# Weight decoding in a fused top-k attention and gated feed-forward kernel: shifts and adds at other places of a slot, the first P@V a slot later, other load counts

## The chip, the cores and the metric

The kernel runs on one core of one Trainium2 chip. The metric is the device time of one execution in microseconds (us); the time of a kernel is the median of its runs. Engines are named as in the profile: PE (TensorE), DVE (VectorE), ACT (ScalarE), POOL (GpSimd) and SP (SyncE). ACT and SP also issue the DMA transfers here.

## The reference

Attention in which every query keeps only its 32 largest scores, followed by a feed-forward layer with the activation h cos(h):

```python
B, H, S, D = 8, 8, 576, 64;  top_k = 32
scores = q @ k.T / sqrt(D)                       # per batch and head
kth    = np.partition(scores, -top_k)[..., -top_k]
scores = np.where(scores >= kth, scores, -1e9)
attn   = exp(scores - max);  attn /= attn.sum() + 1e-9
x = (attn @ v) with heads side by side           # 4608 tokens x 512
h = x @ w_in                                     # 512 -> 2048
out = (h * cos(h)) @ w_out                       # 2048 -> 512
```

q, k and v are float32. `w_in` and `w_out` come as 64-bit floats and are turned into 32-bit ones on the chip.

## The kernel before, in words

**Units and slots.** A unit is 128 tokens and one pair of heads. There are 36 token blocks of 128 and 4 head pairs, so 144 units. The order of all instructions is written out by hand: each engine executes its own in the order in which the code emits them. A loop goes through slots; slot `i` searches the largest scores of unit `u = i` on VectorE, makes mask and exponentials of `w`, the unit before, writes out the unit two before (`send`: split into 16-bit halves on GpSimd, a write of `rows` to memory and a transposing read into `pT`, both on SyncE's queue) and, in every even slot, takes two units `z` (3 and 4 before) through attention times values ("P@V": `values` on TensorE, then `take_values`, L486, on VectorE, which normalises into `xT`). `pT` has three buffers. `LAST` is 140; the last four units go through `last_slot`, and a loop after it finishes the feed-forward work.

**Top-k.** The 576 scores of a row are folded into the larger and the smaller of two halves: `rest` on VectorE (L247) and `low` on GpSimd as sum minus larger (`fold_sum` L265, `fold_low` L274). For units in `BUSY`, `low` is made on VectorE instead (`fold_now`, L255). MAX8 (L352) and MATCH_REPLACE8 (L357) then pull out eight values at a time; round 3 ends a slot on VectorE.

**Scores.** `scores` (L226) of two units are made in one even slot, of one unit where a block crosses a batch; `scored` holds which. ScalarE takes them out of PSUM (`take_scores`, L236 and L237). L237 and P@V use the same PSUM tile `rim`.

**Weights.** The 32 chunks of weights (16 of `w_in`, 16 of `w_out`, 512 KB each as 64-bit floats) are loaded by `load_weights(n, queue)` into staging tiles and decoded in three steps: `decode_first` on ScalarE (L133, L136) at the end of a slot, `decode_second` on VectorE (a shift, L144), `decode_third` on GpSimd (an add, L154). A staging tile is free once the add is done. The counter `wq["ready"]` is the number of chunks whose adds have been emitted before the slot begins. Staging tiles share their seven buffers (`CHUNKS`, tag `g`) with the feed-forward tiles `g`; a load is put off when staged chunks and live `g` tiles would be more than seven. A few early chunks use spare buffers of the tag `x`.

**Feed-forward items.** The work of a token block is cut into 8 first-layer items (`ff1`: 8 matmuls, 16 records of L537, 256 columns of one PSUM bank `mm`) and 8 second-layer items (`ff2`: 2 matmuls, 4 records of L612, all eight accumulated into one bank `o`), 576 items in all. `feed(n)` emits up to n items where the slot calls it, three times a slot, as far as `credit` allows (5 a slot less 0.9 for each unit scored, at most 5.3 kept). Kinds alternate, two first-layer and two second-layer items in turn; when the kind whose turn it is may not go, the other goes and the alternation starts anew from it:

```python
            for kind in (ff["kind"], 1 - ff["kind"]):
                if (can_first, can_second)[kind]():
                    break
            else:
                return
            ...
            if kind != ff["kind"] or ff["half"]:
                ff["kind"], ff["half"] = 1 - kind, 0
            else:
                ff["half"] = 1
```

`can_first` asks for the block's `xT` (two ticks old; a tick is one call of `feed`) and for `wq["ready"]` to cover the chunks of `w_in`; `can_second` asks for gated `g` tiles that are two or three ticks old and for

```python
wq["ready"] >= NC * NF // FC + f + 2     # 16 + f + 2, f = 0, 2, ... 14
```

Both kinds take their PSUM bank from the tag `mm`, which has two buffers. Two first-layer items in turn (even and odd) fill one bank; ScalarE then takes it out (`take_first`: L551, L553) where `take_banks` stands in the code. A bank `o` stays open over its eight second-layer items and is taken out by L622. From a finished `g` tile, GpSimd (L573, L582), ScalarE (a sine, L592) and GpSimd again (`gate`, L599) make h cos(h).

**ScalarE's order in a slot.** In an odd slot from slot 12 on: sine, mask (L381, L383), finished banks, `take_scores`, exponentials (L391), and at the end of the slot finished banks again. In an even slot the exponentials stand ahead of `take_scores`. A sine and an exponential need different activation tables, so an odd slot loads a table twice.

Of the kernel before, what the change touches and what calls it, by code (L numbers as in the profile page):

```python
# [30 lines left out]
def kernel(  # L31
# [16 lines left out]
    NP = H // 2  # L48
# [43 lines left out]
        w_out.append(w)  # L92
        chunks.append((moe_w_out[f * P : (f + 1) * P, :], w))
    CHUNKS, XB = 7, 4
    BUSY = range(7, 12)
    ff = {"live": 0, "tick": 0, "now": 0, "credit": 0.0, "end": False, "kind": 0, "half": 0, "open": 0, "late": False}

    wq = {"next": 0, "loaded": deque(), "second": deque(), "third": deque(), "done": 0, "ready": 0}
# [4 lines left out]
    def load_weights(n, queue):  # L103
        for _ in range(n):
            i = wq["next"]
            if i >= len(chunks):
                return
            src, dst = chunks[i]
            if not DECODE:
                queue.dma_start(out=dst, in_=src)  # L110
                wq["next"] = wq["done"] = i + 1
                continue
            spare = i < 3 * XB and i % 2 == 1 and staged(1) < XB
            if spare:
                st = ffw.tile([P, CW, 2], I32, tag="x", name="st", bufs=XB)
            elif staged() + ff["live"] >= CHUNKS:
                return
            else:
                st = ffw.tile([P, CW, 2], I32, tag="g", name="st", bufs=CHUNKS)
            queue.dma_start(out=st.rearrange("p w i -> p (w i)"), in_=src)  # L120
            wq["loaded"].append((st, dst, int(spare)))
            wq["next"] = i + 1
# [16 lines left out]
    def decode_second(n):  # L139

        for _ in range(min(n, len(wq["second"]))):
            st, w, spare = wq["second"].popleft()
            wi = w.bitcast(I32)
            nc.vector.tensor_scalar(  # L144
                out=wi, in0=wi, scalar1=3, scalar2=None, op0=ALU.logical_shift_left
            )
            wq["third"].append((st, w, spare))
# [13 lines left out]
    units = []  # L161
    for t0 in range(0, B * S, P):
        parts = []
        for i, a in enumerate((t0, t0 + TAIL)):
            b, q0 = a // S, a % S
# [75 lines left out]
    def fold_high(u):  # L241

        s, sc = u["s"], u["sc"]
        if u["n"] not in BUSY:
            del u["sc"]
# [5 lines left out]
    def fold_now(u):  # L251

        s, sc = u["s"], u.pop("sc")
        u["low"] = work.tile([P, 2, HS], F32, tag="low", name="low", bufs=1)
        nc.vector.tensor_tensor(  # L255
            out=u["low"], in0=sc[:, :, 0:HS], in1=s[:, :, HS:S], op=ALU.min
        )

    def fold_sum(u):

        if not u["folds"]:
            return
        s = u["s"].bitcast(I32)
        u["low"] = work.tile([P, 2, HS], F32, tag="low", name="low", bufs=1)
        nc.gpsimd.tensor_tensor(  # L265
            out=u["low"].bitcast(I32), in0=s[:, :, 0:HS], in1=s[:, :, HS:S], op=ALU.add
        )

    def fold_low(u):

        if not u["folds"] or u["n"] in BUSY:
            return
# [19 lines left out]
    def topk_first(u, w):  # L292
# [5 lines left out]
        if u["folds"]:  # L298
            if u["n"] not in BUSY:
                fold_sum(u)  # L300
# [3 lines left out]
        if merges:  # L304
            merge_second(w)
        if u["folds"] and u["n"] in BUSY:
            fold_now(u)
        topk_round(u, 0, [lambda: bounds(w), lambda: distances(w)] if w else ())

    def topk_round(u, rnd, between=(), ahead=None):  # L310
        top, rest, lasts = u["top"], u["rest"], TOPK // 8 - 1
        end = TOPK - 1 - 8 * rnd
        at = top[:, :, end : end - 8 if rnd < lasts else None : -1, 0]
        if u["folds"]:
            search(
                at, rest[:, :, HS:S] if rnd == 0 else rest[:, :, 0:HS], rest[:, :, 0:HS], rnd < lasts,
                between if rnd < lasts else (),
            )
        else:
            search(at, u["s"] if rnd == 0 else rest, rest, rnd < lasts, between)  # L320
        if rnd < lasts:
            return
        del u["rest"]
        if u["folds"]:
            low = u.pop("low")
            for k in range(TOPK // 16):
                more = k < TOPK // 16 - 1
                if ahead and not more:
                    take_values(ahead)
                search(  # L330
                    top[:, :, 1 + 8 * k : 9 + 8 * k, 1], low, low, more,
                    () if more or rnd < lasts else between,
                )
# [10 lines left out]
    def merge_second(u):  # L344
        nc.vector.tensor_reduce(
            out=u["top"][:, :, TOPK - 1, 1], in_=u.pop("lesser"), axis=mybir.AxisListType.X,
            op=ALU.max,
        )

    def search(to, src, rest, more, between=()):  # L350
        for j in range(2):
            nc.vector.max(to[:, j], src[:, j])  # L352
            if between:
                between[j]()
        if more:
            for j in range(2):
                nc.vector.match_replace(rest[:, j], to[:, j], src[:, j], NEG)  # L357
# [39 lines left out]
    def sums(u):  # L397
        den = small.tile([P, 2], F32, tag="den", name="den")
        nc.vector.tensor_reduce(out=den, in_=u["den"], axis=mybir.AxisListType.X, op=ALU.add)
        u["den"] = den  # L400

    def reciprocal(u):
        u["rden"] = small.tile([P, 2], F32, tag="rden", name="rden")
        nc.vector.reciprocal(u["rden"], u.pop("den"))

    def both(u):
        return [lambda: sums(u), lambda: reciprocal(u)] if u else ()
# [71 lines left out]
    def take_values(us):  # L479
        blk, hp, n = block_of[us[0]["tok"]], us[0]["hp"], len(us)  # L480
        if "xT" not in blk:
            blk["xT"] = work.tile([P, NP, P], F32, tag="xT", name="xT", bufs=5)
        for i, u in enumerate(us):
            to, o, pT = blk["xT"][:, hp + i], room[0][:, i * P : (i + 1) * P], u.pop("pT")
            if u["paired"]:
                nc.vector.tensor_tensor(out=to, in0=o, in1=pT[:, 2 * NT + 1], op=ALU.mult)  # L486
            else:
                nc.scalar.copy(out=to, in_=o)
        blk["left"] -= n
        blk["tick"] = ff["tick"]  # L490
# [181 lines left out]
    LAST = NU - NP  # L672
# [7 lines left out]
    at_slot, at_once = {}, {}  # L680
# [7 lines left out]
    for n in range(NP, len(order)):  # L688
        i = last[order[n - 5]] if n >= 5 else 0
        load_at(max(i, 2 * NP + 2), load_qk, *order[n])  # L690
        i = last_values[order[n - 6]] if n >= 6 else 0
        load_at(max(i + 4 - i % 2, 2 * NP + 2), load_v, *order[n])

    for hp in range(NP):
        at_once[hp] = [(load_v, 0, hp)]
    for hp in range(2, NP):
        at_once[hp - 2].append((load_qk, 0, hp))

# [10 lines left out]
        transposes(x)  # L709

    def slot(i, u, w, x, z):
        n = (3, 4, 3, 2)[i] if i < NP else 2 if i < 2 * NP else 3
        if i < NP:
            for load, b, hp in at_once[i]:
                load(b, hp)
        load_weights(n, nc.sync if i < 2 else nc.scalar)
        if x:
            send(x)
        decoding = i < 3 * NP
        ff["late"] = False  # L720
        topk_first(u, w)
        fold_low(u)
        topk_round(u, 1)
        topk_round(u, 2)
        if decoding:
            sines(1)
            gate(1)
        decode_second(NP)
        decode_third()
        reduce_first()  # L730
        reduce_second()
        made = scored.get(i, [])
        if z:
            take_banks()
        feed(1)

        for m in made:
            scores(m)
        if z:
            values(z)  # L740


        late = len(made) > 0

        if i % 2 and not decoding:
            sines(1)
        if w:
            mask(w)
        take_banks()
        if w and late:  # L750
            exponentials(w)
        take_scores(units[i + 1])
        if w and not late:
            exponentials(w)
        topk_round(u, 3, both(w), z)
        ff["late"] = not decoding
        if i in at_slot:
            load, b, hp = at_slot[i]
            load(b, hp)
        gate(1)  # L760
        feed(1 if len(made) == 2 else 2)
        take_banks()
        decode_first(NP)
        reduce_first()
        reduce_second()
        feed(1 if len(made) == 2 else 3)
        if i == LAST:
            sines(1)
# [51 lines left out]
    for i in range(NU + 1):  # L820
        ff["end"] = i >= NU
        ff["credit"] = min(ff["credit"] + 5.0 - 0.9 * len(scored.get(i, [])), 5.3)
        ff["now"] += 1
        wq["ready"] = wq["done"]
        u, w = (units[i - n] if 0 <= i - n < NU else None for n in range(2))
        x = units[i - 2] if 0 <= i - 2 < LAST else None
        z = units[i - 4 : i - 2] if i % 2 == 0 and 0 <= i - 4 < LAST else None
        if i <= LAST:
            slot(i, u, w, x, z)
        else:  # L830
            last_slot(i, u, w, x, z)
# [47 lines left out]
```

## Time and profile before

| | us |
|---|---|
| median of 3 runs | 1460.86 (1460.59 to 1464.63) |
| profiled execution | 1461.65 |
| its span | 1459.9 |
| PE busy | 1386.9 (95%) |
| DVE busy | 1363.8 (93%) |
| POOL busy | 1157.5 (79%) |
| ACT busy | 1088.2 (75%) |

The numbers of the prediction come from this one profiled execution. A row of the timeline gives start, duration, engine, line, operation, the tiles written and read, their shapes and how often it comes in a row; a bracket at its end gives idle time of the engine before it and what ended that. A row of busy time by stage gives the stretch, its length, the busy time of PE, of its weight loads, of DVE, ACT and POOL with their numbers of instructions, the granted clock of TensorE as a share of full speed, the share of DMA and GB/s. Ends of matmuls are modelled, so items are timed from start to start.

### The profile page before, as it was taken

How to read it: one execution, taken by the hardware profiler on the slowest of the kernel's cores; microseconds unless marked ns; L12 is line 12 of the kernel's file. 1: busy time of each engine (PE TensorE's matmuls, PEld its weight loads, DVE VectorE, ACT ScalarE, POOL GpSimd, SP SyncE). 2: the span in 40 equal slices, each digit the busy share in tenths (PEclk: the TensorE clock that was granted, in tenths of full speed). 3: DMA queues.
4: the chain of work that ended last, by engine and by line, in shares of the span. 5: the costliest groups of instructions: out<-in, count | busy, mean ns of one | idle time of the engine just before them, and what ended most of it. 6: DMA issues, size and time to landing. Idle time of an engine off the chain costs nothing.

```text
span 1459.9 us, 30230 instructions
## 1 busy us (share of the span) xinstructions
PE 1386.9 (95%) x10288; PEld 996.8 (68%) x10288; DVE 1363.8 (93%) x5213; ACT 1088.2 (75%) x1910; POOL 1157.5 (79%) x812
## 2 busy tenths in 40 slices
PE   4387899999999999999999999999999999999998
PEld 2265667777777767777777776777777777777665
DVE  7999999999999999999999999999999999999821
ACT  5787767877777777778777777777777787877641
POOL 5867878888888888888888887888888888888410
PEclk6598999999999999999999999999999999999999
DMA  8986687666665576657655666657665566655300
GB/s 254 282 235 192 175 183 182 155 161 190 179 159 152 168 180 169 161 144 201 185 168 143 144 180 182 170 149 185 192 169 144 152 171 168 166 152 152 62 8 15
DMA packets 427434, 240.00 MB, mean 164 GB/s; under 512 B 375952, under 2 KB 392592, under 8 KB 427280
## 3 DMA queue, kind: packets, MB, share of 16 engines
q1 hardware_dynamic: 418704, 216.88, 57.0%
q10 hardware_dynamic: 8576, 21.19, 4.1%
q8 instruction: 81, 1.33, 0.4%
q14 instruction: 73, 0.60, 0.1%
HBM read 45.09 MB, written 101.19 MB: 100 GB/s over the span
## 4 chain that ended last, share of the span: by engine, by line
PE 82%; DVE 8%; ACT 4%; DMA 3%; POOL 1%; issue 1%; SPq 1%; ACTq 0%; POOLq 0%
PE mm L537 31%; PE o L612 31%; PE rim L477 10%; PE sc L226 7%; DVE top L352 4%; DVE rest L357 2%; PE rim L226 2%; DMA v<-in_v_dram 1%; ACT s L391 1%; ACT s L383 1%; DMA k<-in_k_dram 1%; ACT L391 1%; DMA st<-in_moe_w_in_dram 1%; DVE rest L247 1%; DVE low L357 0%
## 5 line engine op out<-in xcount | busy, mean ns | idle before, releaser
L537 PEld LDWEIGHTS mm<-xT,w_in 128*128 128x128 f32 x4608 | 537.0, 192 | 74.8 <-issue 64.7
L612 PE MATMUL o<-w_out,g 128*128 128x512 f32 x1152 | 538.1, 600 | 12.0 <-POOL w_out L154 7.7
L537 PE MATMUL mm<-xT,w_in 128*128 128x128 f32 x4608 | 540.1, 275 | 6.8 <-ACT x L553 3.9
L352 DVE MAX8 top<-rest 128x8 f32<-128x288 f32 x1148 | 480.7, 454 | 0.0
L424 POOL COPY halves<-s 128x2304 uint16<-128x2304 uint16 x140 | 294.8, 2105 | 149.5 <-ACT s L391 149.1
L357 DVE MATCH_REPLACE8 rest<-top,rest 128x288 f32<-128x288 f32 (+1 forms) x860 | 377.0, 446 | 0.0
L612 PEld LDWEIGHTS o<-w_out,g 128*128 128x128 f32 x1152 | 202.4, 190 | 199.0 <-issue 184.2
L352 DVE MAX8 top<-low 128x8 f32<-128x288 f32 x568 | 240.0, 448 | 0.1
L391 ACT ACTIVATE s<-s,nd 128x576 f32<-128x576 f32 x288 | 220.2, 767 | 0.8
L383 ACT ACTIVATE s<-s,top 128x576 f32<-128x576 f32 x288 | 206.1, 766 | 0.0
L274 POOL TENSOR_TENSOR low<-low,rest 128x576 int32<-128x576 int32 x137 | 193.6, 1413 | 10.7
L265 POOL TENSOR_TENSOR low<-s 128x576 int32<-128x576 int32 x137 | 193.7, 1414 | 6.1 <-ACT s L237 4.9
L226 PE MATMUL sc<-k,q 64*128 64x448 f32 (+1 forms) x640 | 157.9, 591 | 36.8 <-DMA k<-in_k_dram 14.9
L551 ACT ACTIVATE g<-mm 128x512 f32<-128x512 f32 x144 | 85.8, 596 | 128.8 <-PE mm L537 124.6
L582 POOL TENSOR_TENSOR x<-g,x 128x1024 f32<-128x1024 f32 x68 | 160.9, 2366 | 5.7
L477 PE MATMUL rim<-pT,v 128*64 128x128 f32 (+1 forms) x2560 | 159.5, 269 | 2.8 <-DMA pT<-rows 2.8
L599 POOL TENSOR_TENSOR g<-g,x 128x1024 f32<-128x1024 f32 x68 | 161.0, 2367 | 1.3 <-ACT x L592 1.3
L477 PEld LDWEIGHTS rim<-pT,v 128*64 128x64 f32 x2560 | 132.8, 139 | 13.1 <-issue 4.0
L236 ACT COPY s<-sc 128x896 f32<-128x896 f32 x144 | 129.2, 897 | 3.9 <-PE sc L226 3.4
L237 ACT COPY s<-rim 128x256 f32<-128x256 f32 x144 | 55.1, 382 | 91.9 <-PE rim L477 91.9
L357 DVE MATCH_REPLACE8 low<-top,low 128x288 f32<-128x288 f32 x284 | 123.6, 443 | 0.0
L226 PEld LDWEIGHTS sc<-k,q 64*128 64x128 f32 (+1 forms) x640 | 47.5, 183 | 100.2 <-DVE rest L357 47.0
(59 smaller groups left out, 1335.8 us busy)
## 6 DMA issues: line engine op xcount, KB each, us to landing
rows<-halves SPq DMA_DIRECT2D x140, 640.0 KB, 3.0
out_dram<-ob ACTq DMA_DIRECT2D x36, 256.0 KB, 2.4
q<-in_q_dram SPq DMA_DIRECT2D x31, 288.0 KB, 3.9
v<-in_v_dram SPq DMA_DIRECT2D x32, 256.0 KB, 3.4
st<-in_moe_w_out_dram ACTq DMA_DIRECT2D x16, 512.0 KB, 5.1
st<-in_moe_w_in_dram SPq DMA_DIRECT2D x10, 512.0 KB, 6.9
k<-in_k_dram SPq DMA_DIRECT2D x31, 144.0 KB, 3.8
k<-in_k_dram SPq DMA_DIRECT2D x32, 128.0 KB, 3.8
```

Of the source, the lines that this page charges most:

```text
L226: nc.tensor.matmul(to[r0 : r0 + rows, j, 0 : k1 - k0], st["q"][d, q0 : q0 + rows], st["k"][d, k0:k1], start=True, stop=True,)
L265: nc.gpsimd.tensor_tensor(out=u["low"].bitcast(I32), in0=s[:, :, 0:HS], in1=s[:, :, HS:S], op=ALU.add)
L274: nc.gpsimd.tensor_tensor(out=low, in0=low, in1=u["rest"][:, :, HS:S].bitcast(I32), op=ALU.subtract)
L352: nc.vector.max(to[:, j], src[:, j])
L357: nc.vector.match_replace(rest[:, j], to[:, j], src[:, j], NEG)
L383: nc.scalar.activation(out=s[:, j], in_=s[:, j], func=AF.Prelu, bias=less[:, j, 1:2], scale=1.0, alpha=FAR)
L391: nc.scalar.activation(out=s[:, j], in_=s[:, j], func=AF.Exp, bias=nd[:, j : j + 1], scale=SCALE, accum_out=den[:, j, 0:1],)
L424: nc.gpsimd.tensor_copy(out=halves[:, :, 0 : 2 * S], in_=s.rearrange("p (k h) -> p h k", h=2))
L477: nc.tensor.matmul(o[d, to], lhsT, rhs, start=c == 0, stop=c == NT)
L537: nc.tensor.matmul(mm[:, at : at + w], w_in[f // FC][:, c, (f % FC) * P : (f % FC + 1) * P], blk["xT"][:, c], start=c == 0, stop=c == NC - 1,)
L599: eng.tensor_tensor(out=g, in0=g, in1=x, op=ALU.mult)
L612: nc.tensor.matmul(o, g[:, at : at + P], w_out[f], start=f == 0, stop=f == NF - 1)
```

## The change

Unit 7 leaves `BUSY`. The values of head pair 3 are loaded in slot 2 instead of slot 3. `load_weights` is called with other counts. The first P@V, of units 0 and 1, is made in slot 5 instead of slot 4; those after it stay where they were. From slot 7 on (`early` is false), `decode_second` is called after the last round of the search instead of before it, and since `decode_third` stays where it is, the add of a chunk is emitted one slot after its shift.

```diff
-    BUSY = range(7, 12)
+    BUSY = range(8, 12)
...
     for hp in range(NP):
-        at_once[hp] = [(load_v, 0, hp)]
+        at_once.setdefault(min(hp, 2), []).append((load_v, 0, hp))
     for hp in range(2, NP):
         at_once[hp - 2].append((load_qk, 0, hp))
...
     def slot(i, u, w, x, z):
-        n = (3, 4, 3, 2)[i] if i < NP else 2 if i < 2 * NP else 3
+        n = (3, 3, 3, 2, 2, 2, 3, 3, 3)[i] if i <= 2 * NP else 2
+        early = i < 2 * NP - 1
         if i < NP:
-            for load, b, hp in at_once[i]:
+            for load, b, hp in at_once.get(i, ()):
                 load(b, hp)
         load_weights(n, nc.sync if i < 2 else nc.scalar)
...
         if decoding:
             sines(1)
             gate(1)
-        decode_second(NP)
+        if early:
+            decode_second(NP)
         decode_third()
...
         topk_round(u, 3, both(w), z)
+        if not early:
+            decode_second(NP)
         ff["late"] = not decoding
...
         x = units[i - 2] if 0 <= i - 2 < LAST else None
-        z = units[i - 4 : i - 2] if i % 2 == 0 and 0 <= i - 4 < LAST else None
+        z = units[i - 4 : i - 2] if i % 2 == 0 and NP < i < LAST + 4 else None
+        if i == NP + 1:
+            z = units[0:2]
```

## The prediction

> **What bounds the kernel now.** I read the granted clock and the busy time by stage first, then the timelines of TensorE and ScalarE over one pair of slots in the middle, then the places where TensorE waits. I cut the span by the start of L247 on VectorE, which opens a slot. Slots 0 to 19 end at 216.98 us, slot 140 starts at 1345.95. Busy time by stage (stretch, length, each engine's busy us, clock, DMA):
>
> ```profile
> 0.00:82.00 82.00, 35.56 (x181) 23.27 (x182) 71.88 (x272) 52.98 (x101) 58.74 (x58) 0.60 0.90 260
> 82.00:207.00 125.00, 108.27 (x809) 77.02 (x809) 121.00 (x448) 96.26 (x172) 97.59 (x69) 0.96 0.73 200
> 207.00:1356.00 1149.00, 1148.66 (x8725) 831.24 (x8724) 1128.28 (x4397) 891.79 (x1555) 981.70 (x671) 1.00 0.63 166
> 1356.00:1460.00 104.00, 94.42 (x580) 65.22 (x578) 42.59 (x100) 47.17 (x83) 19.43 (x16) 1.00 0.09 25
> ```
>
> VectorE sets the pace to 207 us (121.00 of 125.00). After it TensorE is full (1148.66 of 1149.00) with VectorE only 20 us behind. The last 104 us are the backlog of feed-forward items. So the time is TensorE's work plus every hole in it, and the middle, 60 pairs of slots of 18.69 us, weighs most. One such pair on TensorE:
>
> ```profile
> 405.10 1.88 PE L612 MATMUL o<-w_out,g 128*128 128x512 f32 x4
> 406.91 1.02 PE L226 MATMUL sc<-k,q 64*128 64x448 f32 x4
> ...
> 409.06 1.09 PE L477 MATMUL rim<-pT,v 128*64 128x128 f32 x16
> ...
> 411.39 1.98 PE L612 MATMUL o<-w_out,g 128*128 128x512 f32 x4
> 413.21 3.73 PE L537 MATMUL mm<-xT,w_in 128*128 128x128 f32 x32
> 416.78 3.60 PE L612 MATMUL o<-w_out,g 128*128 128x512 f32 x8
> ```
>
> By starts: one second-layer item 1.81 us, scores 2.15, P@V 2.33, two first-layer items 3.57, two second-layer items 3.44. First-layer items come two by two, both halves of one PSUM bank, and two second-layer items stand between a finished bank and the next one begun. ScalarE at the turn from the even to the odd slot of this pair:
>
> ```profile
> 411.90 1.28 ACT L592 ACT_TABLE_LOAD   x1
> 413.19 1.15 ACT L592 ACTIVATE x<-x,halfpi 128x1024 f32<-128x1024 f32 x1
> 415.35 0.20 ACT L381 ACTIVATE nd<-nd 128x2 f32<-128x2 f32 x1 [1.01 <-DVE nd L374]
> ...
> 416.98 0.60 ACT L551 ACTIVATE g<-mm 128x512 f32<-128x512 f32 x1
> ...
> 418.05 0.91 ACT L236 COPY s<-sc 128x896 f32<-128x896 f32 x1
> ...
> 419.25 1.28 ACT L391 ACT_TABLE_LOAD   x1
> 420.54 0.78 ACT L391 ACTIVATE s<-s,nd 128x576 f32<-128x576 f32 x1
> ...
> 422.07 0.57 ACT L622 ACTIVATE ob<-o 128x512 f32<-128x512 f32 x1
> ```
>
> By starts: sine with its table 2.35, mask 1.63 (L381, L383), eviction 1.07, score copies 1.20, table 1.29, exponentials 1.53.
>
> Where a first-layer item does follow a finished bank directly (items 5 and 6 of block 1, issued in slot 12), TensorE waits for the eviction:
>
> ```profile
> 145.80 2.05 PE L537 MATMUL mm<-xT,w_in 128*128 128x128 f32 x16
> 149.12 2.05 PE L537 MATMUL mm<-xT,w_in 128*128 128x128 f32 x16 [1.27 <-ACT x L553]
> ```
>
> Start to start 3.32 us instead of 1.79: a direct neighbour costs 1.5 us with ScalarE free.
>
> **The change, part by part.** The order of the items is fixed by the counters in the code (weights `ready`, staged tiles, credit, tick). Followed slot by slot they give the order that TensorE's timeline of before shows (slot 8: first-layer, scores, P@V, two second-layer; slot 11: first, second, three first); the order after is counted in the same way.
>
> *Unit 7 leaves BUSY.* VectorE loses one L255 (0.67 us by starts at 82.33); GpSimd gains L265 and L274, 1.41 each, in a slot (81.57 to 91.86) where it is busy only 4.5 of 10.3 us. Worth -0.7.
>
> *v of pair 3 a slot sooner.* Its three issues (some 2.7 us of SyncE, 25.47 to 28.2 for the pair before) come before unit 0's rows in slot 2; SyncE was free to 30.90. In slot 3 the rows of unit 1 no longer queue behind them. Nothing on VectorE waits for either: 0.
>
> *First P@V in slot 5.* The 0.8 us that VectorE waited in slot 4 for L486 goes. In return unit 3's transpose needs the buffer that units 0 to 2 all hold until slot 5's L486, so SyncE holds it from 68.06 to about 70; behind it only slot 6's rows (73.34) are queued. P@V of unit 3 (76.60) has 1 to 2 us of slack left. -0.8, or 0 if that slack is used up.
>
> *Shifts.* There are 32 before and after. Three of them stood behind a GpSimd operation:
>
> ```profile
> 97.12 2.37 POOL L599 TENSOR_TENSOR g<-g,x 128x1024 f32<-128x1024 f32 x1
> ```
> ```profile
> 98.14 1.97 DVE L144 TENSOR_SCALAR w_out<-w_out 128x512 int32<-128x512 int32 x2
> ```
>
> Single shifts of slots 8, 10 and 12 took 1.63, 2.58 and 0.57 us beside 0.41 undisturbed, 3.5 us too much in all. Behind the last MAX8 GpSimd does gates and reductions as well, so the gain lies between 3.5 and a loss of the same size; I take -1.5. Fewer items in slots 13 to 18 also free some of the 3.9 us that VectorE waited there, less 1.6 where slot 15 now packs five first-layer items before slot 16's scores. The ramp to slot 20 in all: -4 us (-9 to +4).
>
> *Adds a slot later.* Here is the price. A chunk now stays staged a slot longer, and staged chunks plus live g tiles may not exceed 7. In slot 8 three chunks await the shift's slot, three the add, one g lives: no load. The new counts (3, 3, 3, 2, 2, 2, 3, 3, 3, then 2) ask for the last chunk in slot 11, but loads are refused again in slots 11, 14 and 15. `ready` at the start of slots 7 to 13 was 19, 21, 23, 26, 28, 31, 32; it becomes 18, 18, 21, 24, 24, 26, 28, then 28, 29, 31, 31, 31, and 32 only in slot 19. Second-layer items of block 0 need up to 32. Items issued by the end of slots 8, 12, 16, 18 and 19: before 9, 22, 36, 43, 48; after 7, 21, 31, 32, 37. From there both issue 8 a pair (credit allows 8.2), so 11 items of 576 stay behind to the tail: 11 x 1.72 = +19 us (their time in the chain: 32 records in 13.75 us).
>
> *The phase.* The starved slots shift the alternation by one. By slot 19 an odd number of first-layer items is out (27, before 28). Items still alternate two and two, but now as second half of one bank, first half of the next. An even slot runs second | scores, P@V | first (ends a bank) | first (begins one), an odd one second | second, first (ends) | first (begins), second. The `mm` tag has two banks and an open `o` holds the other, so every begin waits for L551 and L553 of the bank just ended, twice a pair, to the end. In the odd slot those stand behind the exponentials in ScalarE's queue.
>
> The loop, from ScalarE's last eviction of an even slot on: sine 2.35, mask 1.63, copies 1.20, table 1.29, exponentials 1.53 = 8.00; TensorE meanwhile does first, second, second, first in 7.0 and waits; eviction to its end and start of the next matmul 1.24; then first 1.79, two second 3.44, scores 2.15, P@V 2.33, first 1.79 = 11.50; the even eviction, with 0.2 until it starts, 1.27. Sum 22.0 us. Every second odd slot L622 (0.6) stands ahead of the copies: 22.6. Mean 22.3 against 18.69, 3.6 x 60 pairs = **+217 us**. VectorE, 18.48 busy a pair, then waits, some 0.7 for the odd exponentials and 2.6 at L486 for P@V and L237. GpSimd's sum is 16.1 a pair: no bound.
>
> Bounds of that: both waits at the lone 1.5 give 3.0 a pair, +180; if the odd mask also waits for VectorE's L374, as it does now (1.01 us before 415.35), 4.6 a pair, +277. The counted loop leaves the mask 1.6 us of slack, so I stay at 3.6.
>
> The clock: in 148 to 158.8 us TensorE idled 3.3 of 10.8 us in gaps of 1.3 and 2.2 and kept it, so I leave it at 1.00:
>
> ```profile
> 148.00:158.80 10.80, 7.52 (x42) 5.14 (x42) 9.16 (x36) 10.31 (x17) 9.37 (x7) 1.00 0.66 187
> ```
>
> [...]
>
> *Tail.* Eight more direct neighbours from slot 140 on, 1.5 each, less 1.6 and some of TensorE's other holes there that a longer backlog fills (1.9, 1.7, 1.2, 0.4): +9.
>
> **Sum.** The profiled execution took 1461.65 us (span 1459.9), 0.8 above the median. -4 + 217 + 19 + 9 = +241: 1702.7, and against the median 1702.
>
> **Rivals.**
> *Lag without bad neighbours.* If the alternation falls back in step, only the 11 items count: 1460.9 - 4 + 19 = 1476 us. For it: the slots where one unit alone is scored (17, 88) could shift the parity. Against it: followed through them, the order keeps an odd count. 0.09.
> *Faster.* The shifts' collisions (3.5), L255 (0.7) and slot 4's wait (0.8) go and the backlog is made good: 1456 us. It decides only if no more than two items are lacking at slot 140, that is, if the adds came late by one slot and loads were never refused. For it: VectorE bounds the ramp. Against: the seven staging tiles, counted above. 0.04.
> *The phase, with the clock at half for a quarter of the loops*: 11.5 x 60 / 4 = 172 us more, 1875. The row above speaks against it. 0.04.
> No difference at all (ramp and lag cancel, no neighbours) gets 0.01; a measurement here tells about 0.3% from none.
>
> **Numbers.** The phase has 0.82; its own range runs from 3.0 a pair with the ramp's best (1655) to 4.6 with the ramp's worst (1770). With 15 to 10 us at either end for the tail's sum, 1640 to 1780 holds nearly all of it and leaves out the other cases, 0.18 together. Faster 0.04, same 0.01, slower 0.95.
>
> **What the profile after would show.** TensorE's idle time between slots 20 and 140 some 215 us instead of none, ended by ACT L553 at L537; L551 waiting for nothing in odd slots; VectorE idle at L486 behind L237 some 2.6 us a pair; pairs of 22.0 and 22.6 us in turn. `w_out` loads spread to about slot 16, some slots without any. Wrong, if pairs stay at 18.7 us (then 1476), or if no wait for L553 stands ahead of L537 there.

## The result, and the profile after

The changed kernel takes 1753.76 us (median of 4 runs, 1748.82 to 1757.52) against 1462.74 (1460.59 to 1468.11) for the kernel before on the same chip: a ratio of 1.198, 95% interval 1.193 to 1.203. The prediction was 1702, 1640 to 1780. Ratios here and below leave out one slow run, 1651.41 us in the experiment on the phase alone, whose granted clock was 0.927 (0.967 to 0.972 in the three others). The profiled execution took 1753.73 us, its span is 1751.9.

Cut by the start of L247 as before, slot 20 starts at 228.92 us (216.98 before), slot 140 at 1592.60 (1345.95). So the ramp lost 11.9 us, the 120 slots of the middle 234.7 (1363.68 against 1128.97), the tail 45.4 (159.3 against 113.95). Busy time by stage of the changed kernel (stretch, length, busy us of PE, weight loads, DVE, ACT and POOL, granted clock, DMA share, GB/s):

```profile
0.00:82.00 82.00, 35.54 (x190) 23.90 (x191) 72.75 (x275) 53.09 (x101) 58.79 (x59) 0.63 0.90 263
82.00:228.92 146.92, 107.03 (x797) 84.21 (x795) 131.98 (x481) 103.55 (x184) 108.02 (x76) 0.86 0.68 179
228.92:1592.60 1363.68, 1163.64 (x8576) 821.06 (x8576) 1114.39 (x4321) 880.31 (x1528) 969.75 (x660) 1.00 0.50 138
1592.60:1751.90 159.30, 134.75 (x728) 88.84 (x728) 52.43 (x138) 57.42 (x99) 29.42 (x23) 0.95 0.09 26
```

In the middle the engines do the same work, but TensorE, which was full, is idle for 200 us of it (1363.68 - 1163.64); the other 35 us stand in the rows themselves, since a row of matmuls beside a hole is shown with its full length (2.05 for one first-layer item, 1.79 from start to start before). Three of the long waits there, with what ended them (us in total, times, longest):

```profile
PE mm L537 <- ACT x L553: 176.9, 120, 2.0
DVE xT L486 <- ACT s L237: 170.8, 60, 4.5
DVE den L399 <- ACT s L391: 78.1, 56, 2.2
```

120 waits in 60 pairs of slots: two a pair. One pair on TensorE's timeline:

```profile
469.40 2.05 PE L537 MATMUL mm<-xT,w_in 128*128 128x128 f32 x16 [1.26 <-ACT x L553]
471.29 3.60 PE L612 MATMUL o<-w_out,g 128*128 128x512 f32 x8
474.73 1.95 PE L537 MATMUL mm<-xT,w_in 128*128 128x128 f32 x16
478.34 2.05 PE L537 MATMUL mm<-xT,w_in 128*128 128x128 f32 x16 [1.67 <-ACT x L553]
480.23 3.60 PE L612 MATMUL o<-w_out,g 128*128 128x512 f32 x8
...
488.24 2.05 PE L537 MATMUL mm<-xT,w_in 128*128 128x128 f32 x16
491.56 0.71 PE L537 MATMUL mm<-xT,w_in 128*128 128x128 f32 x4 [1.26 <-ACT x L553]
```

Before, first-layer items stood as `x32`, both halves of one bank. Here each row is `x16`, and after each item that ends a bank the next begins one and waits. ScalarE in the same pair:

```profile
469.37 1.28 ACT L592 ACT_TABLE_LOAD   x1
...
471.72 0.19 ACT L381 ACTIVATE nd<-nd 128x2 f32<-128x2 f32 x1
...
473.14 0.88 ACT L236 COPY s<-sc 128x896 f32<-128x896 f32 x1
...
474.31 1.28 ACT L391 ACT_TABLE_LOAD   x1
...
477.14 0.57 ACT L551 ACTIVATE g<-mm 128x512 f32<-128x512 f32 x1
477.61 0.67 ACT L553 ACTIVATE x<-mm,quarter 128x512 int32<-128x512 f32 x1
```

No bracket anywhere from 469.37 to 477.14: sine, masks, copies, table and exponentials run without a stop, L551 stands behind them, and TensorE's matmul of 478.34 behind L553. The chain of waits that ended last says it in one line, before and after:

```profile
PE 82%; DVE 8%; ACT 4%; DMA 3%; POOL 1%; issue 1%; SPq 1%; ACTq 0%; POOLq 0%
```
```profile
PE 52%; ACT 36%; DVE 7%; issue 3%; DMA 1%; ACTq 1%; POOL 1%; POOLq 0%
```

The ramp shows such a chain already in slot 10. Ahead of it TensorE waits for a bank, and then its granted clock is at half for 5.29 us: the two first-layer items take 6.35 us (3.73 at 413.21 us before). Busy time by stage over them stands beneath; then ScalarE and VectorE:

```profile
110.40 6.35 PE L537 MATMUL mm<-xT,w_in 128*128 128x128 f32 x32 [4.96 <-ACT x L553]
```
```profile
110.40:115.69 5.29, 5.29 (x25) 5.29 (x25) 5.29 (x21) 2.54 (x6) 0.00 (x0) 0.50 0.61 127
```
```profile
116.79 0.60 ACT L551 ACTIVATE g<-mm 128x512 f32<-128x512 f32 x1 [3.85 <-PE mm L537]
```
```profile
128.20 0.49 DVE L486 TENSOR_TENSOR xT<-rim,pT 128x128 f32<-128x128 f32 x2 [4.56 <-ACT s L237]
```

The late first-layer items make the eviction late, the sine, masks, exponentials and score copies queue behind it, and VectorE waits 4.56 us at L486. The slot takes 15.47 us (12.93 before).

### The profile page after: what moved, and what is told of

The parts are those of the page before. It is cut to its first block, busy times and chain, and to the rows that moved or that the text cites. A ratio compares the mean times of both kernels' runs of the same rounds, so it can differ in the third digit from the quotient of the medians.

```text
span 1751.9 us, 30286 instructions
## 1 busy us (share of the span) xinstructions
PE 1441.0 (82%) x10288; PEld 1018.0 (58%) x10288; DVE 1371.6 (78%) x5212; ACT 1094.4 (62%) x1910; POOL 1166.0 (67%) x814
## 4 chain that ended last, share of the span: by engine, by line
PE 52%; ACT 36%; DVE 7%; issue 3%; DMA 1%; ACTq 1%; POOL 1%; POOLq 0%
PE mm L537 19%; PE o L612 16%; PE rim L477 9%; PE sc L226 6%; ACT s L391 6%; ACT s L383 5%; ACT x L553 5%; ACT L391 4%; ACT L592 4%; ACT g L551 4%; ACT s L236 3%; DVE top L352 3%; ACT x L592 2%; PE rim L226 2%; DVE rest L357 1%
## 5 line engine op out<-in xcount | busy, mean ns | idle before, releaser
L537 PE MATMUL mm<-xT,w_in 128*128 128x128 f32 x4608 | 592.3, 283 | 214.4 <-ACT x L553 206.8
L537 PEld LDWEIGHTS mm<-xT,w_in 128*128 128x128 f32 x4608 | 552.3, 195 | 286.7 <-ACT x L553 233.4
L612 PE MATMUL o<-w_out,g 128*128 128x512 f32 x1152 | 528.5, 597 | 28.9 <-ACT ob L622 28.9
L426 POOL COPY halves<-rden 128x256 uint16<-128x256 uint16 x140 | 57.2, 409 | 303.0 <-DVE rden L404 303.0
L274 POOL TENSOR_TENSOR low<-low,rest 128x576 int32<-128x576 int32 x138 | 194.8, 1412 | 10.8
L551 ACT ACTIVATE g<-mm 128x512 f32<-128x512 f32 x144 | 84.6, 588 | 153.3 <-PE mm L537 153.3
L486 DVE TENSOR_TENSOR xT<-rim,pT 128x128 f32<-128x128 f32 x140 | 34.2, 286 | 185.9 <-ACT s L237 180.6
L582 POOL TENSOR_TENSOR x<-g,x 128x1024 f32<-128x1024 f32 x68 | 160.7, 2364 | 5.7
```

Source lines behind the costliest of these rows:

```text
L274: nc.gpsimd.tensor_tensor(out=low, in0=low, in1=u["rest"][:, :, HS:S].bitcast(I32), op=ALU.subtract)
L537: nc.tensor.matmul(mm[:, at : at + w], w_in[f // FC][:, c, (f % FC) * P : (f % FC + 1) * P], blk["xT"][:, c], start=c == 0, stop=c == NC - 1,)
L612: nc.tensor.matmul(o, g[:, at : at + P], w_out[f], start=f == 0, stop=f == NF - 1)
```

## The experiments

The theory: the lateness of the adds turns the alternation of the items by one, so that a PSUM bank is begun directly behind one just ended, and that wait is the price. Rivals: the late place costs by itself; the 11 lacking items cost; another edit does.

**One edit alone.** The kernel before with only the late shift and the late add.

```diff
-        decode_second(NP)
+        if i < 2 * NP - 1:
+            decode_second(NP)
...
         topk_round(u, 3, both(w), z)
+        if i >= 2 * NP - 1:
+            decode_second(NP)
```

> The kernel before with one of the edits alone: from slot 7 on the shift behind the last round, the add a slot later. Counted through the code this gives the same order of items as the kernel after from slot 19 on (37 items out instead of 48, 138 to 140 direct neighbours). Theory: about 1745 us (1730 to 1765). Rival (the edits cost only together: load counts, v, P@V in slot 5): under 1600.

Measured: 1747.17 us (1746.43 to 1748.54), ratio 1.195 [1.192, 1.199]. Its middle takes 1365.35 us against the changed kernel's 1363.68. One edit of five is the loss. By the medians the other four add some 5 to 7 us to it, but the intervals of the two ratios overlap.

**The same edit taken back.** All of the change but the shift, which stands in front of the last round again (`early = True`).

> The kernel after with the shift back in front of the last round in every slot; the other four edits stay. Order of items as before (48 out by slot 19). Theory: 1460 us (1452 to 1468): slots 0 to 4 gain some 4 us as in the trace of after, slot 5 gives about that back. Rival (the other edits carry a good part of the loss): above 1500.

Measured: 1465.4 us (1459.47 to 1469.64), ratio 1.003 [1.001, 1.005]. This is in the theory's range: the other four edits are worth nothing; at most they cost 0.5%.

**Late shift, add in the same slot.**

```diff
         if not early:
             decode_second(NP)
+            decode_third()
```

> The kernel after with the add directly behind the late shift, in the same slot: the shift stays behind the last MAX8, staging and weights ready are as before. Theory (the late add, by staging and phase, is the whole loss): order of items as before, 1460 us (1450 to 1470). Rival (the shift's new place costs, as it stands behind GpSimd's reductions): the shifts and adds there lengthen slots 7 to 12 by 2 to 4 us each, 1475 to 1485, and if it is the whole loss above 1600.

Measured: 1471.67 us (1468.49 to 1475.23), ratio 1.007 [1.004, 1.009]; just above the theory's range and below the rival's. So the late place of the shift without the late add costs some 10 us against the kernel before, of which the kernel with the shift back has some 4 already, and not 291. No item lacks, and the pairs of the middle take 18.7 us; in the profiled execution, the slowest of the six, the loss stands in the ramp (slot 20 at 230.59 us), in slots 8, 10 and 12. Slot 8 on GpSimd, ScalarE and VectorE:

```profile
94.13 3.80 POOL L154 TENSOR_TENSOR w_out<-w_out,st 128x512 int32<-128x512 int32 x3 [6.80 <-issue]
```
```profile
101.43 1.15 ACT L592 ACTIVATE x<-x,halfpi 128x1024 f32<-128x1024 f32 x1 [3.01 <-POOL x L582]
```
```profile
109.09 0.49 DVE L486 TENSOR_TENSOR xT<-rim,pT 128x128 f32<-128x128 f32 x2 [6.38 <-ACT s L237]
```

Three adds at the start of the slot hold GpSimd's L573 and L582 to 101.34; the sine waits 3.01 us for them, everything on ScalarE queues behind the sine, and L486 waits 6.38.

**The phase put right in the changed kernel, first-layer items alone.** A first half of a bank is always followed by its second.

```diff
+            odd = kind == 0 and first[0][1] % 2
...
-            if kind != ff["kind"] or ff["half"]:
+            if kind == 0:
+                ff["kind"], ff["half"] = (1, 0) if odd else (0, 1)
+            elif kind != ff["kind"] or ff["half"]:
```

> The kernel after, with one rule more: the second first-layer item of a bank always follows its first, and then the kind changes. Weights, staging, shifts, adds and the 11 items of lag stay as in the kernel after; only the begin of a bank directly behind the end of another goes (7 such places instead of 138). Theory (bank neighbours): pairs of slots fall from 22.7 back to 18.7 us, 60 x 4.0 = 240 off the middle; the slower ramp (+12) and the lag (11 x 1.72 = 19) stay: about 1495 us (1485 to 1510). Rival (the late adds themselves, or GpSimd's fuller odd slots, slow every slot): above 1700.

Measured: 1591.28 us (1589.05 to 1592.72), ratio 1.088 [1.085, 1.091]: between the two, so both expectations failed. The wait for L553 is gone from the middle, but another has come, every fourth slot:

```profile
PE mm L537 <- ACT ob L622: 65.0, 28, 2.3
```

(28 waits, counted from 260 to 1400 us.) With an odd lag the second-layer items were now out of step: the last item of one block and the first of the next were issued together, the new `o` opened in the second bank while the old `o` waited for L622 behind the exponentials, and the next first-layer pair found no bank. Two of these places on TensorE:

```profile
347.43 3.84 PE L537 MATMUL mm<-xT,w_in 128*128 128x128 f32 x32 [2.32 <-ACT ob L622]
...
387.40 5.47 PE L537 MATMUL mm<-xT,w_in 128*128 128x128 f32 x32 [2.32 <-ACT ob L622]
```

The same wait, but the second pair of items takes 5.47 us: the granted clock is 0.50 from 388.00 us on, for 3.41 us (see the last section). Four slots take 40.0 us, or 41.6 with such a spell, instead of 37.4.

**Both kinds by banks.** So the rule was extended: second-layer items go in twos that begin with an even pair of rows.

```diff
             if kind == 0:
+                odd = first[0][1] % 2
                 ff1(*first.popleft())
+                ff["kind"], ff["half"] = (1, 0) if odd else (0, 1)
             else:
+                odd = second[0][2] % 4
                 ff2(*second.popleft())
-            if kind != ff["kind"] or ff["half"]:
-                ff["kind"], ff["half"] = 1 - kind, 0
-            else:
-                ff["half"] = 1
+                ff["kind"], ff["half"] = (0, 0) if odd else (1, 1)
```

> The changed kernel with all its edits, but the alternation tied to the banks for both kinds: the second first-layer item of a mm bank always follows its first, and second-layer items go in twos that begin with an even pair of rows, so that block k's last and block k+1's first are no longer issued together. By the counters the lag stays at 11 items by the end of slot 19, and 7 direct neighbours are left. Theory (the price is a bank begun directly behind one that has just ended, mm or o): pairs of slots near 18.7 us from slot 22 to 139, no wait of L537 for L553 or L622 there, and before + 19 (lag) + 10 (ramp) + 5 (tail) = some 1495 us, 1480 to 1515. Rival (any order other than that of before pays, because L622 stands behind the exponentials whatever the kinds do): a wait of over 1 us in every second odd slot, over 1550 us.

Measured: 1508.96 us (1506.79 to 1511.37), ratio 1.032 [1.029, 1.035], inside the theory's range. All five edits are in, the same 11 items lack, and 243 of 291 us are gone. What is left: ramp +11.1, middle +24.2, tail +14.3 us. So the sum came out in part by luck: the theory had nothing in the middle and 24 us of lag and tail. In the middle a wait for L553 remains every fourth slot, since L622 now stands in that slot's queue ahead of it:

```profile
488.51 3.73 PE L537 MATMUL mm<-xT,w_in 128*128 128x128 f32 x32
492.09 3.60 PE L612 MATMUL o<-w_out,g 128*128 128x512 f32 x8
496.38 3.84 PE L537 MATMUL mm<-xT,w_in 128*128 128x128 f32 x32 [0.69 <-ACT x L553]
```

**The phase alone.** The kernel before with none of the edits; only the alternation is turned.

```diff
-            if kind != ff["kind"] or ff["half"]:
+            if kind == 0:
+                ff["kind"], ff["half"] = (0, 1) if odd else (1, 0)
+            elif kind != ff["kind"] or ff["half"]:
```

> The kernel before with none of the five edits; only the alternation is turned by one item, so that a first-layer item that ends a mm bank is followed by the one that begins the next. By the counters no item is lacking by the end of slot 19 (48, as before), and there are 110 direct neighbours. Theory (the phase is the price, whatever brings it about): 110 waits at the 1.75 us that one cost in the changed kernel (235 us of the middle over some 130 neighbours) = +190, 1650 us (1600 to 1690), while the ramp to slot 20 and the tail stay within 6 us of before. Rival (the lateness of the chunks is what costs, the phase only accompanies it): 1461, at most 1475.

Measured: 1630.46 us (1625.97 to 1651.41), ratio 1.114 [1.110, 1.118]. The rival is out: without any late chunk the middle alone loses 138.5 us. The size was near (+169 of 190 expected), its place partly wrong: the middle has three such waits every four slots, which take 42.1 us instead of 37.4, so 1.57 a wait and not 1.75 (and 235 us over the 120 waits of the changed kernel's middle are 1.96 each, not 1.75), and ramp and tail, which were to stay, lost 13.8 and 19.2. TensorE:

```profile
479.79 1.95 PE L537 MATMUL mm<-xT,w_in 128*128 128x128 f32 x16
483.13 3.84 PE L537 MATMUL mm<-xT,w_in 128*128 128x128 f32 x32 [1.39 <-ACT x L553]
488.24 2.05 PE L537 MATMUL mm<-xT,w_in 128*128 128x128 f32 x16 [1.27 <-ACT x L553]
```

**One slot later.** The whole change, but the late place from unit 8 on: `early = i < 2 * NP`.

> The changed kernel with all its edits, but the shifts go behind the last MAX8, and the adds a slot later, from unit 8 on instead of unit 7. By the counters loads are refused in other slots, an even number of first-layer items is out when the weights are all in, 8 direct neighbours are left and 4 items are lacking by the end of slot 19 (44 instead of 48). Theory (the late place costs mainly through the phase that the starved slots happen to leave): 1461 + 7 (4 items x 1.72) + 10 (ramp, as with the add in the same slot) = 1478 us, 1468 to 1492, with pairs of 18.7 us. Rival (late shifts and adds cost by themselves, one slot sooner or later being all the same): over 1650 us.

Measured: 1470.04 us (1467.26 to 1474.44), ratio 1.006 [1.004, 1.007]; theory. The edits are the same, by the counters the loads are refused in other slots, and the parity comes out even. In the middle TensorE is busy for the whole stretch again:

```profile
221.89:1348.54 1126.65, 1126.65 (x8572) 815.10 (x8570) 1108.68 (x4321) 877.99 (x1530) 967.28 (x661) 1.00 0.63 167
```

**What could be kept.** Two kernels asked whether some edit is worth having: the shift back and the first P@V back in slot 4, and the kernel before with the sooner v alone.

> The kernel with the shift back in front of the last round and the first P@V back in slot 4; what stays of the change is unit 7, the sooner v and the new load counts. In the kernel with the shift alone put back, slots 5 and 6 took 24.7 us instead of the 19.7 of before, while slots 1 to 4 took 4.0 less. Theory (P@V in slot 5 only moves the wait: the buffer of the transposes is late there): slots 5 and 6 return to 19.7 and slot 4 to 11.5, so the ramp is 2 to 3 us shorter than before: 1458 us (1454 to 1462). Rival (unit 7 on GpSimd is what made slots 5 to 8 long): 1464 us or more.

> The kernel before with one edit alone: v of pair 3 loaded in slot 2 instead of slot 3. Theory (it only takes SyncE's three issues out of the way of slot 3's rows, and nothing on VectorE waits for either): no difference, 1461 us (1457 to 1465). Rival (the 1.3 us that VectorE waits in slot 2 of before, and is not seen in the changed kernel, go with it): 1459 us.

Measured: 1463.21 us, ratio 1.002 [1.001, 1.004], and 1461.86, ratio 1.002 [1.000, 1.004]. The first lies between its theory and its rival, the second is as the theory had it. In the first, slots 5 and 6 did return to 19.7 us, but slot 4 took 13.31, not 11.5, with VectorE idle 3.03 of it: the first P@V moves the wait from one slot to the other. In both, what the profiled ramp gained (1.2 and 1.7 us to slot 20) is not in the medians. No version beat the kernel before.

## Why the prediction was right, step by step

The mechanism, its place and its cause were as predicted: the refused loads, the last chunk loaded in slot 16, 37 items by the end of slot 19, the odd count, two waits a pair for L553, the odd one behind the exponentials. The total was 52 us short, in these terms:

- *Loop*, 22.3 us a pair, +217: measured 22.73, +234.7. The pair shown is 22.15 long (469.37 to 491.52) where 22.0 were counted: sine to exponentials 7.77 (8.00, the masks took 1.42 instead of 1.63), eviction 1.20 (1.24), but the first-layer item after the hole 1.89 (1.79), the two second-layer items behind it 3.53 (3.44), the last item up to the start of its eviction 2.09 (1.99) and that eviction 1.19 (1.07). Every second pair is 23.25 instead of 22.6: L622 with the wait behind it costs 1.1, not 0.6. VectorE waited 2.8 us a pair at L486 (2.6 forecast) and 1.3 for the exponentials (0.7).
- *Ramp*, -4 (-9 to +4): measured +11.9, outside its bounds. The shifts, -1.5 between 3.5 either way, took 21.4 us instead of 17.7: +3.7, with one of 2.58 in slot 7 beside L582. P@V in slot 5 shortened slot 4 and lengthened slot 5 (13.32, VectorE 2.04 idle behind L274), as its repetition without the late shift shows. The rest stands with the late evictions in slots 10, 12, 16 and 17 (VectorE idle 14.7 us there). The working priced the neighbours from slot 20 on and none before, and it left the clock at 1.00; from 82.00 us to slot 20 it was 0.86 (0.96 before, from 82.00 to 207.00). Ahead of slots 12 and 16, as ahead of slot 10, TensorE waits for a bank and then does two first-layer items partly at half clock (0.69 over the 5.47 us of each pair):

```profile
135.48 5.47 PE L537 MATMUL mm<-xT,w_in 128*128 128x128 f32 x32 [1.91 <-ACT x L553]
...
179.25 5.47 PE L537 MATMUL mm<-xT,w_in 128*128 128x128 f32 x32 [2.71 <-ACT x L553]
```

In the profiled execution of the kernel with the late shift and add alone, the pair ahead of slot 12 took 3.84 us, VectorE idled 0.16 us in slots 10 and 12 together (8.5 here), and slot 20 came only 2.8 us later than before. The kernel with the phase alone lost 13.8 us in the ramp. How the 11.9 divide into phase, place of the shift, the other edits and the clock, no run separates.

- *Lag*, 11 items x 1.72 = +19: in the kernel with both kinds by banks the tail lost 14.3, and TensorE idled less there than before (from slot 141 on 3.94 us, 9.44 before): the longer backlog filled holes.
- *Tail neighbours*, +9: eleven waits for L553 stand in the tail, 17.8 us, where the working had eight more neighbours, less some holes filled. TensorE's idle time from slot 141 on rose by 14.8 us (24.22), and behind four of its holes the clock went to half (0.50) for 3.41 us each, some 7 us together (an estimate, half of 4 x 3.41):

```profile
1617.48 3.68 PE L537 MATMUL mm<-xT,w_in 128*128 128x128 f32 x16 [2.41 <-ACT x L553]
```

- *v sooner*, 0, and *unit 7*, -0.7: nothing to be seen above the scatter, with the four edits together at +0.3%.

Of the rivals, "lag without bad neighbours" (1476) needed a parity that falls back; the kernel that starts one slot later is close to that case, with 4 items behind instead of 11, at 1470. The lower end of the phase's own range, 1655, adds up to 1660 (1461 - 9 + 180 + 19 + 9). The clock at half in the loop did not come: over the middle it was 1.00. The working took 1.00 from a single row of before (148.00 to 158.80 us, idle for 3.3 of 10.8); in the kernel with first-layer items by pairs it fell to 0.50 behind one hole of 2.32 us and not behind another (see the last section).

## What to carry to other kernels

Where two kinds of work alternate by counters over two buffers, which item follows which is part of the schedule: a delay that costs nothing where it stands can shift the parity, and then the price comes at every turn to the end. Follow the counters over the whole start before moving a step that feeds them, and tie the alternation to the buffers, for all kinds that share them, not to a count. An eviction behind a long queue on its engine is harmless only as long as nobody needs that buffer before the queue ends; here TensorE's waits for L553 came to 176.9 us in the middle.

## What the hardware showed beside that

In the kernel with first-layer items by pairs, the 28 holes of 2.32 us between 260 and 1400 us had two outcomes. One of each is shown above: the holes that end at 347.43 and at 387.40 us. Busy time of two stretches of 3.41 us, one behind the other, at each:

```profile
343.63:347.04 3.41, 1.48 (x4) 0.38 (x2) 3.19 (x12) 3.38 (x8) 1.07 (x2) 1.00 0.59 104
347.04:350.45 3.41, 3.02 (x27) 3.02 (x28) 3.41 (x15) 0.34 (x1) 3.41 (x3) 1.00 0.68 192
384.59:388.00 3.41, 1.09 (x7) 0.60 (x6) 3.20 (x13) 2.75 (x6) 1.07 (x2) 1.00 0.88 192
388.00:391.41 3.41, 3.41 (x19) 3.41 (x18) 3.41 (x16) 0.00 (x0) 3.33 (x4) 0.50 0.55 221
```

Behind the first hole the clock stayed at 1.00; behind the second it was 0.50 from 388.00 to 391.41 us. Over the 13.41 us from the start of each hole TensorE was busy for the same 11.09 us, with a clock of 1.00 (345.11 to 358.52) and of 0.87 (385.08 to 398.49). So the length of the hole alone does not decide it; what does is not shown here. In the changed kernel's middle, through 120 holes of 1.26 to 2.02 us (three of them above 1.74), the clock stayed at 1.00.
